# A table of 1152 scale factors, transposed on TensorE before it is written to memory

## The chip, the core and the metric

The kernel runs on one core of a Trainium2 chip. Its engines work side by side, each through its own queue in order: TensorE (PE) multiplies matrices into PSUM banks, VectorE (DVE) and ScalarE (ACT) do elementwise work, GpSimd (POOL) issues the gathers and scatters by index, SyncE (SP) issues the other transfers. All transfers run on the same 16 DMA engines. The metric is the device time of one execution in microseconds (us); lower is better.

## The reference

Attention over (2, 8, 576, 64), then a first mixture of eight experts with Sinkhorn weights, then a second mixture in which each of N = 1152 tokens goes to its best expert alone:

```
xn = x / (norm(x) + 1e-6);  en = emb / (norm(emb) + 1e-6)
logits = xn @ en.T / tau
expert_idx = argmax(logits, 1);  probs = softmax(logits)
gate_w = probs[arange(N), expert_idx]
for e in range(8):
    mask = expert_idx == e
    out[mask] = gate_w[mask, None] * (relu(x[mask] @ w1[e]) @ w2[e])
```

x has 512 columns, w1[e] is 512x1024 and w2[e] 1024x512. The change concerns the factor per token, gate_w with the kernel's own scaling, on its way to the last line.

## The kernel before, in words

The tokens lie nine to a partition (nine tiles of 128), so a number per token is a [128, 9] table. The second mixture first routes (`route`, line 1124, three groups of 384 tokens; `favourite`, line 1208, and `places`, line 1250, turn counts per expert into positions), and then computes in slots of 128 tokens that share an expert. In the profiled execution 11 slots are computed. Each token's row is written to a table in memory, `rows`, and its factor to another, `sizes`. A slot then fetches what belongs to it by index: `gather` (line 1328) its 128 rows into a tile in `nb`, `size` (line 1338) its 128 factors into a tile `sz`. Both are issued by POOL through `fetch` (line 1344). Rows of the slots 0 to 2 are turned round on PE (`transposed`, line 1102: eight small matmuls from `nb`, then one copy by ACT into a tile in `r_e`); from slot 3 on a transposing transfer on SP does it.

A slot (`slot`, line 1350) has two halves on PE. The ups multiply by w1 (96 matmuls 128x128, two PSUM banks), ACT and DVE turn their result into a high and a low fp16 half in `xa`. The downs multiply by w2 (18 matmuls 128x512 in fp16, and the last two blocks in fp32, which the trace shows as rows `r_k,xa`) into a third bank. ACT then writes the result times the token's factor (`x<-pb,sz`) and POOL scatters it to `out`. Weights come over SP (`r_st`, `r_e`, `r_k` from `in_m2w`, line 1306), skipped where the slot has the expert of the slot before, and are split into halves by ACT (high) and DVE (low) into `r_bias`, `r_q`, `r_v`, `r_e`.

`scales` (line 1192) makes the factors from row sums, the logits and their maxima: `norm_inverse`, an Exp on ACT, a sum, two reciprocals. `sizes` is needed first by the gather of slot 0's factors, and so by the end of slot 0.

The order on the engines is not the order of the code. Every call is recorded and `Plan.issue` (line 268) issues the operations of a whole stage by estimated costs and due times, keeping the best of several rounds. The first mixture, the routing and the first 11 slots are one such stage, so an added operation can move others far from it. PSUM banks are taken in turn from a ring of six (`turn_of(banks)`), slot after slot. All recorded instructions carry the line 157, so rows are told apart by their tiles.

Of the kernel before, what the change touches and what calls it, by code (L numbers as in the profile page):

```python
# [10 lines left out]
F32 = mybir.dt.float32  # L11
F16 = mybir.dt.float16
BF16 = mybir.dt.bfloat16
I32 = mybir.dt.int32
# [8 lines left out]
N, DM, E, F = 1152, 512, 8, 1024  # L23
NT = 9
# [298 lines left out]
def attn_moe_moe_kernel(ctx: ExitStack, tc: tile.TileContext, a, out):  # L323
    nc = tc.nc
    vec, act, pe, pool, sp = nc.vector, nc.scalar, nc.tensor, nc.gpsimd, nc.sync
# [4 lines left out]
    def sbuf_pool(name, bufs, stack=ctx):  # L330
        return stack.enter_context(tc.tile_pool(name=name, bufs=bufs))
# [3 lines left out]
    sml = sbuf_pool("sml", 1)  # L335
# [4 lines left out]
    vec, act, pe, pool, sp = (plan.engine(e) for e in "vatgs")  # L340
# [20 lines left out]
    def carve(t, *parts, off=0):  # L361

        out = []
        for shape, dtype in parts:
            out.append(at(t, off, shape, dtype))
            off += -(-int(np.prod(shape)) * mybir.dt.size(dtype) // 64) * 64
        return out
# [3 lines left out]
    def turn_of(ring):  # L371
        i = turns[id(ring)] = turns.get(id(ring), -1) + 1
        return ring[i % len(ring)]
# [72 lines left out]
    def take(n):  # L446
        nonlocal o
        o += n
        return cst[:, o - n:o]

    ident, upper, desc8, iotas = take(128), take(128), take(8), take(SLOTS)
    steps, lower8, iota128, numbers = take(72), take(64), take(128), take(18).rearrange("p (t i) -> p t i", i=2)

    def tt(eng, out, in0, in1, op=ALU.add):
        eng.tensor_tensor(out=out, in0=in0, in1=in1, op=op)
# [14 lines left out]
    def warm(ps, n):  # L470
# [10 lines left out]
        out=sst, in0=w2r.unsqueeze(1).to_broadcast([128, 4, H]), in1=blk4.unsqueeze(2).to_broadcast([128, 4, H]),  # L481
# [568 lines left out]
    def norm_inverse(nrm, inv, ss, tmp):  # L1050

        rsqrt(inv, tmp, ss, 3)
        tt(vec, nrm, ss, inv, ALU.mult)
        vec.tensor_scalar(nrm, nrm, 1e-6, None, ALU.add)
        vec.reciprocal(inv, nrm)

    zr = at(hss[1], 2048, [DM], I32)[0:1]
    emb, upper16, ones16, rank, st2, lt, order8, wk, w8, w16, en = carve(
        r_e, ([DM], F32), ([128], F16), ([128], F16), ([NT, E], F32), ([8, NT], F32), ([3, NT, E], F32),
        ([E, E], F32), ([NT, E], F32), ([E, E], F32), ([2, SLOTS, E], F32), ([KD, E], F32), off=r_sml)  # L1060
# [4 lines left out]
    rows = drp.tile([N + 1, DM], I32, name="rows")  # L1065
    sizes = drp.tile([N + 1, 1], I32, name="sizes")
    szs = [sml.tile([128, 1], I32, name=f"sz{i}") for i in range(4)]
    seen = sml.tile([128, E], F16, name="seen")
    oh = sml.tile([128, NT, E], F16, name="oh")
    fav = sml.tile([128, 3, E], F32, name="fav")  # L1070
# [121 lines left out]
    def scales():  # L1192

        norm_inverse(st2[:, 1], st2[:, 6], st2[:, 0], st2[:, 7])
        l = lt[:, 2]
        tt(vec, l, lt[:, 0], st2[:, 4].unsqueeze(2).to_broadcast([128, NT, E]), ALU.subtract)
        tt(vec, l, l, st2[:, 6].unsqueeze(2).to_broadcast([128, NT, E]), ALU.mult)
        act.activation(l, l, ACTF.Exp)
        vec.tensor_reduce(out=st2[:, 7], in_=l, axis=AX.X, op=ALU.add)
        vec.tensor_scalar(st2[:, 7], st2[:, 7], 1e-9, C_XN * C_W * C_W, ALU.add, ALU.mult)  # L1200
        tt(vec, st2[:, 7], st2[:, 7], st2[:, 2], ALU.mult)
        vec.reciprocal(st2[:, 7], st2[:, 7])
        with nc.allow_non_contiguous_dma(reason="a number per token"):
            sp.dma_start(out=sizes[0:N, 0].rearrange("(t p) -> p t", p=128), in_=st2[:, 7].bitcast(I32))

    got, xn_early = [], []

# [179 lines left out]
    mps, banks = [scs[2][:, 0:512]], [scs[0][:, 0:512], scs[1][:, 0:512], pab, pO]  # L1387
# [50 lines left out]
    for _ in route(2):  # L1438
        pass
    scales()  # L1440
    got += [xn_early[0], size(0)]

# [65 lines left out]
```

## Time and profile before

| | before |
|---|---|
| median of three runs | 1100.46 us (1097.18 to 1105.92) |
| the profiled execution | 1098.71 us, of it span 1096.9 us |
| PE busy, of the span | 1027.2 us, 94% |
| DVE, ACT, POOL busy | 842.3, 702.4, 288.6 us |
| mean granted TensorE clock | 0.976 |

A row of the timeline has start, duration, engine, line, operation, and the tiles as out<-in with shape and count. A bracket at its end gives the engine's idle time just before it and what ended that. In the stage tables each engine has its busy time with the count of instructions; PEclk is the granted share of TensorE's 2.4 GHz, so 0.50 is the lower level, 1.2 GHz.

### The profile page before, as it was taken

To read this page: it belongs to the slowest core of one execution; us is meant where nothing else is said; L and a number is where in the kernel's file an instruction comes from. 1 tells how busy PE (TensorE), PEld (TensorE's weight loads), DVE (VectorE), ACT (ScalarE), POOL (GpSimd) and SP (SyncE) were. 2 spreads that over 40 slices of the span, in tenths; PEclk is the share of its full clock that TensorE was granted. 3 is DMA by queue.
4 is the path that set the end of the run, shared out by engine and by line. 5 is a ranking of instruction groups with operands and counts; after the bars stand their busy time and mean duration, and the time that the engine had idled before them with its cause. 6 is when DMAs were issued, how large, how long until landed. Compare 5 with 4: busy or idle time off the path is not lost. (4 is left out here: it accounts for less than half of the span.)

```text
span 1096.9 us, 28775 instructions
## 1 busy us (share of the span) xinstructions
PE 1027.2 (94%) x11973; PEld 909.2 (83%) x11973; DVE 842.3 (77%) x1366; ACT 702.4 (64%) x1119; POOL 288.6 (26%) x233
## 2 busy tenths in 40 slices
PE   6787999999899999999999999999999999859896
PEld 2344666799899999999999999999999999636563
DVE  7887888756767697787787787887887887957882
ACT  6777999931436467576576576566666665657872
POOL 3452000001642132232332232222322210154221
PEclk9789999999999999999999999999999999979999
DMA  8644234200577057257357357348345023257693
GB/s 279 180 141 124 54 78 110 95 2 19 149 177 172 14 141 167 64 136 169 67 128 174 68 119 169 78 112 178 79 122 114 2 85 117 70 96 212 184 295 101
DMA packets 79472, 132.71 MB, mean 121 GB/s; under 512 B 19030, under 2 KB 40222, under 8 KB 79080
## 3 DMA queue, kind: packets, MB, share of 16 engines
q1 hardware_dynamic: 61432, 95.94, 28.5%
q0 software_dynamic: 17904, 34.88, 18.3%
q8 instruction: 95, 1.56, 0.6%
q14 instruction: 41, 0.34, 0.1%
HBM read 111.87 MB, written 5.29 MB: 107 GB/s over the span
## 5 line engine op out<-in xcount | busy, mean ns | idle before, releaser
L157 PEld LDWEIGHTS <-r_bias 128*128 128x128 f16 x4920 | 400.5, 98 | 7.3 <-issue 6.6
L157 PEld LDWEIGHTS <-r_v 128*128 128x128 f16 x2880 | 235.7, 98 | 6.8 <-issue 5.7
L157 PE MATMUL pb<-r_k,r_bias 128*128 128x192 f16 x2304 | 205.0, 247 | 0.5 <-ACT r_e L157 0.5
L157 POOL TENSOR_TENSOR r_q<-r_w,r_q 128x768 f16<-128x768 f32 (+1 forms) x54 | 107.7, 1994 | 268.4 <-ACT r_q L157 262.3
L157 PE MATMUL pb<-nb,r_v 128*128 128x192 f16 x1260 | 151.4, 246 | 0.7 <-ACT r_e L157 0.7
L157 PE MATMUL pb<-r_q,r_bias 128*128 128x192 f16 x1512 | 132.8, 246 | 0.0
L157 PE MATMUL pb<-nb,r_e 128*128 128x192 f16 x756 | 103.6, 246 | 0.0
L157 PE MATMUL pb<-xa,r_v 128*128 128x192 f16 x1008 | 99.5, 246 | 0.0
L157 PEld LDWEIGHTS <-r_e 128*128 128x128 f16 x1139 | 95.7, 98 | 1.2 <-issue 1.1
L157 ACT ACTIVATE r_e<-pb 128x384 f32<-128x384 f32 (+1 forms) x96 | 48.1, 504 | 63.8 <-PE pb L157 63.3
L157 ACT ACTIVATE r_w<-pb 128x384 f32<-128x384 f32 x96 | 46.5, 487 | 54.9 <-PE pb L157 54.4
L157 PEld LDWEIGHTS <-r_q 128*128 128x128 f16 (+1 forms) x560 | 41.4, 101 | 43.0 <-issue 21.2
L157 POOL DMA_DIRECT2D r_st<-r_st x42 | 42.3, 1008 | 116.0 <-DMA r_st<-in_m1w 49.9
L157 DVE TENSOR_TENSOR r_q<-r_w,r_q 128x384 f16<-128x384 f32 (+1 forms) x46 | 65.4, 1421 | 5.2 <-ACT r_q L157 5.1
L157 DVE CUSTOM_DVE_ANT_0 r_e<-sc,nb 128x576 f32<-128x576 f32 x72 | 53.7, 754 | 15.0 <-PE sc L157 11.8
L157 ACT ACTIVATE r_bias<-r_bias,r_w 128x576 f32<-128x576 f32 x72 | 59.5, 859 | 8.6 <-DVE r_bias L157 3.4
L157 POOL DMA_DIRECT2D r_e<-r_e x42 | 41.2, 980 | 87.3 <-DMA r_e<-in_m1w 43.2
L157 ACT ACTIVATE r_q<-r_w 128x1152 f16<-128x1152 f32 x50 | 57.8, 1156 | 4.8 <-DMA r_w<-in_qT 4.8
L157 ACT ACTIVATE r_e<-r_e,mn 128x576 f32<-128x576 f32 x72 | 55.4, 770 | 8.4 <-DVE mn L157 8.1
L157 PE MATMUL pab<-r_bias,r_w 128*32 128x288 f32 x472 | 46.6, 446 | 14.1 <-DVE r_bias L157 11.0
L157 DVE SCALAR_TENSOR_TENSOR r_bias<-r_st,r_bias 128x1024 f16<-128x1024 f32 (+1 forms) x45 | 50.5, 1138 | 11.8 <-ACT r_bias L157 11.6
L157 ACT ACTIVATE r_bias<-r_st 128x1024 f16<-128x1024 f32 (+1 forms) x45 | 43.4, 985 | 21.6 <-PE pb L157 17.8
(238 smaller groups left out, 1990.9 us busy)
## 6 DMA issues: line engine op xcount, KB each, us to landing
r_k<-in_m2w SPq DMA_DIRECT2D x48, 512.0 KB
r_st<-in_m2w SPq DMA_DIRECT2D x24, 512.0 KB
r_e<-in_m2w SPq DMA_DIRECT2D x24, 512.0 KB
r_st<-in_m1w SPq DMA_DIRECT2D x22, 512.0 KB
r_st<-in_m1w SPq DMA_DIRECT2D x42, 256.0 KB
r_e<-in_m1w SPq DMA_DIRECT2D x42, 256.0 KB
r_e<-in_m1w SPq DMA_DIRECT2D x14, 512.0 KB
r_st<-r_st POOLq DMA_DIRECT2D x14, 512.0 KB, 6.3
```

The lines of the kernel that those rows point to most:

```text
L157: self.add(e, lambda: f(*a, **k), cost, dma, ins, outs, port)
```

## The change

The [128, 9] table of factors is first transposed on PE into a bank of the ring, as [9, 128]; DVE copies it to a new tile `szt`, and SP writes that: nine runs of 128 numbers, 512 bytes each. Before, SP wrote straight from the [128, 9] table, where neighbours in a row lie 512 bytes apart in memory: 1152 runs of 4 bytes. What stands in memory is the same.

```
     szs = [sml.tile([128, 1], I32, name=f"sz{i}") for i in range(4)]
+    szt = sml.tile([NT, 128], F32, name="szt")
...
         vec.reciprocal(st2[:, 7], st2[:, 7])
-        with nc.allow_non_contiguous_dma(reason="a number per token"):
-            sp.dma_start(out=sizes[0:N, 0].rearrange("(t p) -> p t", p=128), in_=st2[:, 7].bitcast(I32))
+        ps = turn_of(banks)[0:NT, 0:128]
+        pe.transpose(ps, st2[:, 7], ident)
+        vec.tensor_copy(szt, ps)
+        sp.dma_start(out=sizes[0:N, 0].rearrange("(t p) -> t p", p=128), in_=szt.bitcast(I32))
```

The transpose takes one bank of the ring, so every slot's banks move on by one, and the planner's order changes too. Three places matter.

PE, from the end of the routing to the first rows of slot 2. `pb<-r_w,x` are the nine matmuls of `places` from which every later index follows, `pb<-r_e,...` the ups of slot 1, `pb<-r_bias,xa` its downs, `pb<-r_e,nb` the turning of slot 2's rows. Before:

```order
L157 MATMUL pb_3114<-r_e,r_bias 128x128
L157 LDWEIGHTS x_70
L157 MATMUL pb_3115<-r_w,x_70 128x36
L157 LDWEIGHTS xa
L157 MATMUL pb_3109<-r_bias,xa 128x512
...
L157 MATMUL pb_3109<-r_k_76,xa 128x512 x2
L157 LDWEIGHTS nb_72
L157 MATMUL pb_3116<-r_e,nb_72 128x128
```

The same place now (`pb_3111<-r_e 9x128` is the new transpose, `pb_3114<-r_k_76,xa` the end of slot 0's downs):

```order
L157 MATMUL pb_3114<-r_k_76,xa 128x512
L157 LDWEIGHTS x_70
L157 MATMUL pb_3116<-r_w,x_70 128x36
L157 LDWEIGHTS r_q
L157 MATMUL pb_3115<-r_e,r_q 128x128
...
L157 MATMUL pb_3111<-r_e 9x128
...
L157 LDWEIGHTS nb_72
L157 MATMUL pb_3117<-r_e,nb_72 128x128
...
L157 LDWEIGHTS xa
L157 MATMUL pb_3111<-r_bias,xa 128x512
```

The nine matmuls have moved from the end of slot 1's ups to a place before them, beside slot 0's downs (which moved behind the counting of the routing), and slot 2's rows are turned before slot 1's downs instead of after them.

ACT, where it copies slot 2's turned rows (`r_e<-pb 128x1024`). Before:

```order
L157 ACTIVATE xa<-pb_3114 128x256
L157 ACTIVATE r_bias<-r_st 128x2x512
L157 ACTIVATE r_q<-r_st 128x2x512
L157 ACTIVATE r_q<-r_e 128x2x512
L157 ACTIVATE r_v<-r_e 128x2x512
L157 ACTIVATE r_e<-pb_3116 128x1024
L157 ACTIVATE r_v<-r_k_75 128x2x512 x3
```

And now:

```order
L157 ACTIVATE xa<-pb_3110 128x256
L157 ACTIVATE r_e<-pb_3117 128x1024
L157 ACTIVATE r_bias<-r_st 128x2x512
L157 ACTIVATE r_q<-r_st 128x2x512
L157 ACTIVATE r_q<-r_e 128x2x512
L157 ACTIVATE r_v<-r_e 128x2x512
L157 ACTIVATE r_v<-r_k_75 128x2x512 x3
```

The copy has moved ahead of the four splits of slot 2's w1.

SP, where it writes the table (ISA rows set registers). Before:

```order
L1306 DMA r_e<-in_m2w 128x1024
L157 DMA sizes<-r_e 128x9x1
L1306 ISA
L1306 DMA r_k_75<-in_m2w 128x2x512
L1306 ISA
```

And now:

```order
L1309 DMA r_e<-in_m2w 128x1024
L1309 ISA
L1309 DMA r_k_75<-in_m2w 128x2x512
L157 DMA sizes<-szt 9x128
L1309 ISA
```

The write stands one weight load later. On POOL the gathers keep their order up to slot 3's factors: two early gathers of rows, seven more, then the factors of the slots 0 to 3.

## Rows read from the trace of the kernel before

**Rows 1.** Stages of the span: length, then busy time of the engines.

```profile
300.00:929.00 629.00, 625.72 (x7571) 624.14 (x7569) 496.21 (x609) 389.05 (x580) 176.91 (x131) 1.00 0.49 115
929.00:986.00 57.00, 41.57 (x465) 31.99 (x462) 42.09 (x114) 34.85 (x54) 17.98 (x14) 0.88 0.42 89
986.00:1087.00 101.00, 94.18 (x956) 64.15 (x954) 76.17 (x75) 70.25 (x91) 27.87 (x19) 0.98 0.70 209
```

**Rows 2.** Timeline of PE, from slot 1's turned rows to slot 2's downs.

```profile
948.73 0.62 PE L157 MATMUL pb<-r_e,nb 128*128 128x128 f16 x8 [2.23 <-DMA nb<-rows,idx_early]
950.46 0.33 PE L157 MATMUL pb<-r_e,r_q 128*128 128x128 f16 x3 [1.11 <-ACT r_e L157]
...
956.29 4.04 PE L157 MATMUL pb<-r_bias,xa 128*128 128x512 f16 x18
960.17 1.88 PE L157 MATMUL pb<-r_k,xa 128*128 128x512 f32 x4
970.56 1.04 PE L157 MATMUL pb<-r_e,nb 128*128 128x128 f16 x8 [8.51 <-DMA nb<-rows,idx]
972.71 0.48 PE L157 MATMUL pb<-r_e,r_bias 128*128 128x128 f16 x3 [1.11 <-ACT r_e L157]
...
981.98 2.42 PE L157 MATMUL pb<-r_v,xa 128*128 128x512 f16 x6 [2.38 <-ACT x L157]
```

**Rows 3.** Timeline of POOL: gathers of rows for slots 1 and 2.

```profile
944.47 1.87 POOL L157 DMA_INDIRECT nb<-rows,idx_early  x1 [28.13 <-DVE r_e L157]
957.48 1.00 POOL L157 DMA_INDIRECT nb<-rows,idx  x1 [11.14 <-ACT xa L157]
```

**Rows 4.** Timeline of SP: three row stores ahead of slot 1's gather; the table's write.

```profile
937.64 3.83 SPq L157 DMA_DIRECT2D rows<-nb  x3
...
957.64 0.39 SPq L157 DMA_DIRECT2D sizes<-r_e  x1
```

**Rows 5.** Packets from 958 to 960 us by queue: packets, MB, share of 16 engines.

```profile
q0 software_dynamic: 7, 0.03, 113.1%
q1 hardware_dynamic: 1168, 0.00, 26.2%
```

**Rows 6.** All packets from 960 to 962 us.

```profile
DMA packets 0, 0.00 MB, mean 0 GB/s; under 512 B 0, under 2 KB 0, under 8 KB 0
```

**Rows 7.** All packets from 962 to 969 us.

```profile
DMA packets 56, 0.20 MB, mean 29 GB/s; under 512 B 7, under 2 KB 7, under 8 KB 56
```

**Rows 8.** All packets from 972 to 973 us.

```profile
DMA packets 125, 0.39 MB, mean 389 GB/s; under 512 B 30, under 2 KB 30, under 8 KB 125
```

**Rows 9.** PE alone in two stretches: length, PE busy, granted clock.

```profile
965.25:975.49 10.24, 3.81 (x35) 0.50 0.77 163
982.32:985.73 3.41, 3.41 (x10) 0.50 0.21 79
```

**Rows 10.** Timeline of DVE: first and last step of the chain that makes the indices.

```profile
946.62 0.16 DVE L157 COPY fav<-pb 128x8 f32<-128x8 f32 x1
...
956.55 0.19 DVE L157 TENSOR_SCALAR idx<-pb 128x36 int32<-128x36 f32 x1
...
956.88 0.21 DVE L157 RECIPROCAL r_e<-r_e 128x9 f32<-128x9 f32 x1
```

**Rows 11.** Timelines of PE and DVE: another table transposed and copied earlier in the kernel.

```profile
269.27 0.27 PE L157 MATMUL sc<-r_e 128*72 128x128 f32 x1
...
269.58 0.29 DVE L157 COPY r_e<-sc 72x128 f32<-72x128 f32 x1 [0.68 <-PE sc L157]
```

**Rows 12.** Timelines of ACT (copy and three splits) and DVE (one split).

```profile
971.64 1.02 ACT L157 ACTIVATE r_e<-pb 128x1024 f16<-128x1024 f16 x1 [10.73 <-PE pb L157]
972.56 2.94 ACT L157 ACTIVATE r_v<-r_k 128x1024 f16<-128x1024 f32 x3
...
958.10 1.22 DVE L157 SCALAR_TENSOR_TENSOR r_bias<-r_st,r_bias 128x1024 f16<-128x1024 f32 x1 [0.52 <-ACT r_bias L157]
```

**Rows 13.** Waits of ACT from 986 to 1087 us, the largest for weights: total, times, longest.

```profile
ACT r_v L157 <- DMA r_e<-in_m2w: 3.5, 4, 1.9
```

## Prediction: what the transposed table does to the time

> **What bounds the kernel now.** I read the stages first [rows 1]. From 300 to 929 us, the bulk of the first mixture, PE is busy 625.72 of 629.00 us: whatever the changed order does there, it can win at most 3.3 us. From 986 us to the last slot PE is busy 94.18 of 101.00 us. Between them lies the one loose stretch, 929 to 986 us, where the routing ends and the slots begin: 41.57 of 57.00 us, 15.4 us idle.
>
> PE's timeline names these 15.4 us [rows 2]. Five waits make 15.3 of them: 2.23 for slot 1's gathered rows, 1.11 for their copy, 8.51 for slot 2's rows, 1.11 for their copy, 2.38 for ACT's scaling of slot 0. The reader is to see the 8.51: PE has finished slot 1's downs at 962.05 (960.17 + 1.88) and starts the next matmul at 970.56.
>
> Why are slot 2's rows late? POOL issued their gather at 957.48; slot 1's gather, issued at 944.47, let PE go on at 948.73 [rows 2, 3]. The same 256 KB took 13.1 us (970.56 - 957.48) against 4.3. Between the issue and the data of the slow one lies SP's write of the table at 957.64 [rows 4]. The queues show what it does. From 958 to 960 us 1168 packets of at most 512 bytes start on SP's queue, and 7 packets of the gather are recorded with 113.1% of 16 engines' time over 2 us: 1.131 x 32 / 7 = 5.2 us each, where they overlap the write [rows 5]. Then not one packet starts for 2 us [rows 6], for the next 7 us the engines move 29 GB/s [rows 7], and at 972 us they move 389 GB/s [rows 8]. The gathers queued by then cannot fill that time: seven would be 1.8 MB, five microseconds at that rate. The engines look as if they wait for 1152 writes of 4 bytes to be finished, and everybody behind them waits too.
>
> The stall costs more than its length. TensorE's granted clock is 0.50, the 1.2 GHz level, from 965.25 to 975.49, with 3.81 us of work in it, and again from 982.32 to 985.73 with 3.41 us, after PE had idled 8.51 and then 2.38 us [rows 2, 9]. At 2.4 GHz these 7.22 us would have been half: 1.9 and 1.7 us lost.
>
> **The change part by part.** Nothing else is taken out: the 1152 runs become nine of 512 bytes. SP's sequencer spent 0.39 us on the old write; this is not on the path.
>
> *The stall.* With the write gone, the gather should take the 4.3 us of slot 1's. The new order also asks for it differently: the nine matmuls that end in `idx` stand before slot 1's ups, the rows are turned right after these ups. From `idx` to the gather's issue it took 0.93 us (956.55 to 957.48) [rows 3, 10], so the rows are there 5.2 us after `idx`; slot 1's ups take 950.46 to 956.29, 5.8 us less a few tenths for the matmuls woven into them [rows 2]. So the wait goes to about nothing: -8.5, and -1.9 for the clock after it.
>
> *The moved index chain.* From the first counts on DVE to `idx` it is 9.9 us (946.62 to 956.55) [rows 10]. Before, slot 1's turned rows and ups and 3.3 us of waits lay beside it. Now PE has only slot 0's downs (5.8 us, as slot 1's: 956.29 to 962.05) and the turned rows of slot 1 (0.6 us): 9.9 - 6.4 = 3.5 us of waiting, in which the wait for slot 1's gather is contained, plus about 1 us by which the counting, moved forward, waits for DVE. An estimate from these rows: 4.5 us instead of 3.3, +1.2. Bounds: -1 (DVE's chain loses the few operations that the new order puts behind it) and +3.
>
> *The new operations.* A transpose of 72 columns took 0.27 us on PE, its copy 0.29 us on DVE after 0.68 us of waiting [rows 11]; this one has 9 columns. PE pays +0.3. The write follows later by about a microsecond, but it is short: the last of three stores of rows ended its issue at 941.47 and the gather that needs it began at 944.47, so 256 KB in full rows were visible 3.0 us later [rows 3, 4]. The factors' gathers stand behind seven gathers of rows on POOL, so they find them there.
>
> *ACT's moved copy.* The copy (1.02) now precedes four splits (0.98 each on ACT, 1.2 on DVE) that slot 2's ups need [rows 12]. Copy, first ACT split, four DVE splits: 1.0 + 1.0 + 4.8 = 6.8 us, beside 5.8 us of slot 1's downs. PE waits about 1.0 where it waited 1.11 for the copy: 0 (-1 to +1).
>
> *The end of slot 0.* The 2.38 us before slot 2's downs stand for ACT's scaling, which came late because ACT had stood 10.73 us behind the copy [rows 2, 12]. Now ACT reaches it after the copy, nine splits and one half of the ups' result, some 11 us after the turned rows; PE has downs, that 1 us and ups beside it, 12 us. I keep 0.5: -1.9, and -1.7 for the second slow clock. But a wait of 3.5 us ahead of slot 1's ups may itself bring a slow stretch of 3.4 us, which costs 1.7; I charge half, +0.9.
>
> *Given back.* -8.5 - 1.9 + 1.2 + 0.3 + 0 - 1.9 - 1.7 + 0.9 = -11.6. The later slots do not all move up with it. ACT already waits for weights there, 3.5 us in its largest group [rows 13], and an order that is now bound by loads has only 6.8 us of idle PE in which to absorb them [rows 1]. Bounds 0 and 4; I take +1.8, the middle of a guess on the low side. That leaves -9.8 us. The first mixture's order changes in small pieces; with PE 99.5% busy and no wait to take I count 0, within 1.5.
>
> The profiled execution had 1098.71 us (span 1096.9 and 1.8 around it), 1.75 under the median of 1100.46. From the one the sum gives 1088.9, from the other 1090.7. I say **1090.5 us**, its own range 1087 to 1094.
>
> **The page that speaks against it.** The Trainium skill, "DMA: Bandwidth & Descriptors", section "Queues, rings and completion order", says that each engine goes round-robin between the queues it has work for, a packet at a time. By that rule the gather would have been held up only by packets' own time, and the first rival below follows; here 7 packets of the gather stand for 5.2 us each instead. The Trainium skill, same page, section "Back-pressure in remote DMA", says that stalled writes stall the source engine's other queues too; it is written for transfers between cores, and the silent 2 us [rows 6] agree with it.
>
> **The rivals.**
> *The write is innocent.* Its 1168 packets took 26.2% of 16 engines over 2 us, 0.5 us per engine [rows 5]; taken as what it costs, the 13.1 us belong to seven gathers issued in a row, and the new order only moves them. Then slot 2's rows come 13 us after `idx` and PE waits some 8 us, before slot 1's downs instead of after. Gain 0 to 2: 1099. For it: recorded packet time. Against it: 29 GB/s with nothing else to move [rows 7], and full rate as soon as that ends [rows 8].
> *The gain is given back in the slots.* The stall was also time in which ACT, DVE and the loads fell behind nobody. If the loads of the later slots now come late by 4.2 us more in sum than the 1.8 that I charge, 1090.5 + 4.2: 1095.
> *More than that.* No slow clock ahead of slot 1, nothing given back: 1.8 + 0.9 + up to 1.2: 1086.
> *Slower: PE waits for its new transpose.* It stands in PE's queue after 72 of slot 1's 96 ups, so all that follows waits for the last reciprocal. That came 0.33 us after `idx` [rows 10]; in the new order two splits stand between on DVE, 2.4 us more, against some 4 us of ups (72 of 96, 5.5 in all): 1.3 us of slack. If Exp or those splits make it late by more than that, every further microsecond is PE's; from 11 us on the gain is gone, and 22 us late (22 - 1.3 - 9.8 = 10.9 us more than before) it is 1% slower, 1112. Nothing in the rows is that late.
>
> **How the numbers follow.** The likeliest gets 0.60, of which 0.24 lies beyond 1% (11 us, about what a measurement of this kernel tells from no change). More than that 0.10, innocent write 0.14, given back 0.11, slower 0.05. Faster by over 1%: 0.24 + 0.10 = 0.34. Within 1%: 0.36 + 0.14 + 0.11 = 0.61. Slower: 0.05. The range 1084 to 1098 takes in the likeliest, more, and given back, and leaves out slower and most of the innocent write, under 0.2.
>
> **What would show it.** In the changed profile: no 1168 small packets, slot 2's gather about 4 us from issue to use, no 8.5 us wait before slot 2's turned rows; waits of 3 to 5 us in all around the nine `r_w,x` matmuls; slot 2's downs some 10 us earlier than 981.98; at most one stretch at 0.50 there. The sum is wrong if slot 2's rows are again 10 us or more on their way, if PE stands at `pb<-r_e 9x128`, or if the last hundred microseconds grow by more than 4.

## The result, and the profile after

The changed kernel took 1086.24 us (median of four, 1083.69 to 1088.49) where the kernel before, run beside it, took 1099.95: a ratio of 0.9874, 95% interval 0.9844 to 0.9903, some 13.7 us. Timed again in a later batch it took 1091.78 us (1086.42 to 1093.25) against 1100.84, 0.9902 (0.9868 to 0.9936), 9.1 us. It is about 1% faster; which side of 1% the two batches do not settle.

| | before | after |
|---|---|---|
| the profiled execution | 1098.71 us, span 1096.9 | 1088.49 us, span 1086.6 (the slowest of its four) |
| PE, DVE, ACT busy | 1027.2, 842.3, 702.4 us | 1025.3, 845.6, 702.1 us |
| packets under 512 B | 19030 | 17871 |
| mean granted clock | 0.976 | 0.981 |

The stages of the changed kernel, in the columns of [rows 1]:

```profile
300.00:929.00 629.00, 625.86 (x7568) 623.86 (x7567) 499.07 (x610) 389.07 (x581) 175.75 (x131) 1.00 0.49 115
929.00:986.00 57.00, 51.72 (x575) 39.76 (x573) 48.27 (x121) 40.82 (x62) 23.51 (x17) 0.91 0.34 99
986.00:1087.00 101.00, 84.93 (x848) 57.48 (x846) 69.93 (x70) 64.77 (x84) 23.45 (x17) 0.94 0.68 210
```

The first mixture is what it was (625.86 us of PE work for 625.72). The loose stretch, 929 to 986 us, now holds 51.72 us of work instead of 41.57; the stretch behind it holds less because the kernel ends earlier.

PE's timeline of the changed kernel through that stretch; it answers [rows 2]:

```profile
942.72 0.66 PE L157 MATMUL pb<-r_e,nb 128*128 128x128 f32 x4 [0.25 <-DVE r_e L157]
...
943.91 0.17 PE L157 MATMUL pb<-oh,r_e 128*128 128x8 f16 x1 [0.52 <-DVE oh L157]
...
947.72 2.72 PE L157 MATMUL pb<-r_v,xa 128*128 128x512 f16 x6 [3.37 <-DVE nb L157]
...
960.38 0.27 PE L157 MATMUL pb<-r_e 128*9 128x128 f32 x1
...
961.83 0.61 PE L157 MATMUL pb<-r_e,nb 128*128 128x128 f16 x8
962.27 4.05 PE L157 MATMUL pb<-r_bias,xa 128*128 128x512 f16 x18
...
969.27 0.28 PE L157 MATMUL pb<-r_e,r_v 128*128 128x128 f16 x2 [0.67 <-DVE r_v L157]
...
974.72 4.04 PE L157 MATMUL pb<-r_v,xa 128*128 128x512 f16 x18 [0.47 <-ACT x L157]
```

Read first the two rows without a bracket in the middle: the new transpose (`pb<-r_e 128*9`) and slot 2's turned rows at 961.83. Nothing waits there; the 8.51 us of [rows 2] are gone. Slot 2's downs start at 974.72 instead of 981.98. A new wait stands at 947.72, 3.37 us ahead of slot 0's downs.

The gathers of rows (POOL) and the table's write (SP) of the changed kernel, as in [rows 3, 4]:

```profile
944.76 1.41 POOL L157 DMA_INDIRECT nb<-rows,idx_early  x1 [27.21 <-ACT x L157]
957.09 1.74 POOL L157 DMA_INDIRECT nb<-rows,idx  x1 [10.92 <-DVE idx L157]
```

```profile
961.00 0.35 SPq L157 DMA_DIRECT2D sizes<-szt  x1
```

Slot 2's rows, asked for at 957.09, were in use at 961.83, 4.7 us later, where it had been 13.1. The index that they are fetched by, `idx`, was made as late as before, at 956.62 (DVE):

```profile
956.62 0.20 DVE L157 TENSOR_SCALAR idx<-pb 128x36 int32<-128x36 f32 x1 [2.00 <-PE pb L157]
```

The windows of the changed kernel: the stretch of [rows 7], then the stretches at half clock, as in [rows 9]:

```profile
962.00:969.00 7.00, 6.60 (x40) 3.34 (x37) 4.84 (x5) 6.97 (x9) 5.73 (x5) 1.00 0.81 230
```

```profile
938.72:942.13 3.41, 3.41 (x27) 3.35 (x26) 2.98 (x6) 3.11 (x8) 0.00 (x0) 0.50 0.43 154
945.54:952.37 6.83, 4.66 (x12) 1.58 (x12) 6.80 (x42) 2.49 (x4) 0.63 (x1) 0.50 0.43 155
```

The engines move 230 GB/s where they had moved 29. The half clock has not gone away: in this stage it has moved ahead, to the counting and slot 0's downs.

The spans differ by 10.3 us. Split at slot 2's downs: 7.26 up to there (981.98 to 974.72), 2.6 from there to ACT's last scaling, which starts at 1086.35 before and 1076.50 after (first and second row), and 0.45 in what follows.

```profile
1086.35 0.69 ACT L157 ACTIVATE x<-pb,sz 128x512 f32<-128x512 f32 x1 [3.70 <-issue]
```

```profile
1076.50 0.69 ACT L157 ACTIVATE x<-pb,sz 128x512 f32<-128x512 f32 x1 [3.70 <-issue]
```

### The profile page after: what moved, and what is told of

The parts are those of the page before. It is cut to its first block, busy times and chain, and to the rows that moved or that the text cites. A ratio compares the mean times of both kernels' runs of the same rounds, so it can differ in the third digit from the quotient of the medians.

```text
span 1086.6 us, 28773 instructions
## 1 busy us (share of the span) xinstructions
PE 1025.3 (94%) x11974; PEld 909.0 (84%) x11974; DVE 845.6 (78%) x1367; ACT 702.1 (65%) x1119; POOL 290.6 (27%) x233
## 2 busy tenths in 40 slices
DMA packets 78322, 132.71 MB, mean 122 GB/s; under 512 B 17871, under 2 KB 39072, under 8 KB 77930
## 5 line engine op out<-in xcount | busy, mean ns | idle before, releaser
L157 DVE SCALAR_TENSOR_TENSOR r_bias<-r_st,r_bias 128x1024 f16<-128x1024 f32 (+1 forms) x45 | 50.5, 1137 | 13.3 <-ACT r_bias L157 13.1
```

Of the source, the lines that this page charges most:

```text
L157: self.add(e, lambda: f(*a, **k), cost, dma, ins, outs, port)
```

## The experiments

Eleven runs follow, one of them of the changed kernel again; the four with an additional write have a table of their own further down. "Order" says whether the instructions stand in about the sequence of the kernel before or of the changed one. In the table "gather" is the time from the issue of slot 2's gather on POOL to PE's first use of its rows; where PE did not wait it is an upper bound.

| kernel | the table's write | order | median us | ratio to before | gather us | PE's wait for it |
|---|---|---|---|---|---|---|
| before | 1152 x 4 B, side by side | old | | 1 | 13.1 | 8.51 |
| runs of 36 bytes | 128 x 36 B | old | 1092.29 | 0.9934 [0.9912, 0.9956] | 4.5 | none |
| five of nine columns | 640 x 4 B, side by side | nearly old | 1100.30 | 1.0012 [0.9991, 1.0034] | 11.5 | 6.84 |
| rows of 64 bytes | 1152 x 4 B, 64 B apart | nearly old | 1087.39 | 0.9891 [0.9860, 0.9922] | 4.7 | 0.72 |
| one more turn | 1152 x 4 B, side by side | new | 1092.81 | 0.9945 [0.9923, 0.9968] | 4.6 | none |
| transpose in the other ring | 9 x 512 B | nearly old | 1091.66 | 0.9929 [0.9906, 0.9952] | 3.9 | none |
| changed, other bank for rows | 9 x 512 B | nearly old | 1092.00 | 0.9914 [0.9880, 0.9948] | 3.8 | none |
| changed, again | 9 x 512 B | new | 1091.78 | 0.9902 [0.9868, 0.9936] | 4.8 | none |

### The write alone: 128 runs of 36 bytes, in the order of before

```
-            sp.dma_start(out=sizes[0:N, 0].rearrange("(t p) -> p t", p=128), in_=st2[:, 7].bitcast(I32))
+        sp.dma_start(out=sizes[0:N, 0].rearrange("(p t) -> p t", p=128), in_=st2[:, 7].bitcast(I32))
```

> The kernel before with one line changed: the table's 1152 numbers are written as 128 runs of 36 bytes (each partition's nine together) instead of 1152 runs of 4 bytes. No transpose, no copy, and the order of all instructions on every engine is that of before. What it changes in the computation: a token gets another token's factor. Theory (the 4-byte writes hold up the engines and all that is queued behind them): slot 2's gather takes 4 to 5.5 us from issue to use instead of 13.1, the wait of 8.5 us before slot 2's turned rows shrinks to 0 to 1.5 us, the slow clock behind it goes; 6 to 12 us under the kernel before. Rival 1 (the write is innocent, the new order alone brings the gain): gather 12 to 13 us, wait 8 us, within 2 us of before. Rival 2 (the fewer packets bring the stall's end, but the last hundred microseconds give it back): the wait is gone and the time is less than 5 us under before.

POOL and PE of this kernel:

```profile
959.49 1.00 POOL L157 DMA_INDIRECT nb<-rows,idx  x1 [12.49 <-ACT xa L157]
```

```profile
963.94 0.61 PE L157 MATMUL pb<-r_e,nb 128*128 128x128 f16 x8
...
975.13 5.73 PE L157 MATMUL pb<-r_v,xa 128*128 128x512 f16 x18 [3.95 <-ACT x L157]
```

The gain was 6.9 us, with no instruction moved on any engine. The write made the stall: the innocent write falls. The 8.51 us turn into nothing at slot 2's rows; slot 2's downs start 16.6 us after `idx` (958.55) instead of 25.4. What it does not get rid of is the last wait: 3.95 us for ACT's scaling of slot 0, which waits for its factors, gathered behind seven gathers of rows.

### The order alone: one more turn of the ring, the old write kept

```
         vec.reciprocal(st2[:, 7], st2[:, 7])
+        turn_of(banks)
         with nc.allow_non_contiguous_dma(reason="a number per token"):
```

> The kernel before with one added statement that takes a turn of the ring of PSUM banks and does nothing with it, where the change puts its transpose. The old write of 1152 times 4 bytes stays; the order of the instructions and the banks of the slots become nearly those of the changed kernel. Nothing in the computation changes. Theory (the write makes the stall, the shifted banks make PE wait for `nb<-pb` ahead of slot 0's downs): the stall of 7 to 9 us for slot 2's rows stays, shown wherever the new order puts these rows, and the 3.4 us wait ahead of slot 0's downs appears too; 0 to 5 us slower than before. Rival 1 (the order and the banks bring the gain): no wait over 2 us for slot 2's rows, 8 to 14 us faster than before. Rival 2 (part by part): the order hides some of the stall and gives better later slots: 2 to 5 us faster.

SP, a window, and PE of this kernel:

```profile
964.57 0.39 SPq L157 DMA_DIRECT2D sizes<-r_e  x1
```

```profile
969.00:975.00 6.00, 3.96 (x65) 3.63 (x66) 6.00 (x7) 4.62 (x6) 0.13 (x1) 1.00 0.61 33
```

```profile
948.33 2.72 PE L157 MATMUL pb<-r_v,xa 128*128 128x512 f16 x6 [2.60 <-DVE nb L157]
...
981.22 5.45 PE L157 MATMUL pb<-r_v,xa 128*128 128x512 f16 x18 [4.53 <-ACT x L157]
```

6.4 us faster, so every expectation missed in part. The wait ahead of slot 0's downs appears as the theory said. But in the new order the factors are finished later than `idx`, and the write leaves SP 4.75 us behind slot 2's gather (964.57 after 959.82) instead of 0.16: the gather has its rows by then. The engines still stand, 33 GB/s from 969 to 975 us; weights and the gathers of factors meet it, and PE pays 4.53 us at slot 2's downs. The change therefore did two things, and either alone takes slot 2's gather out of the stall. That is why their gains, 6.9 and 6.4, need not add up; the changed kernel with both was 13.7 us faster in one batch and 9.1 in the other.

### The dose: 640 words instead of 1152

```
         sp.dma_start(out=sizes[N:N + 1], in_=zr[:, 0:1])
+        sp.dma_start(out=sizes[640:N, 0].rearrange("(o n) -> o n", o=1), in_=zr)
...
-            sp.dma_start(out=sizes[0:N, 0].rearrange("(t p) -> p t", p=128), in_=st2[:, 7].bitcast(I32))
+            sp.dma_start(out=sizes[0:640, 0].rearrange("(t p) -> p t", p=128), in_=st2[:, 7, 0:5].bitcast(I32))
```

> The kernel before with 640 of the 1152 numbers written (five of the nine columns); the other 512 entries get zeros in one 2 KB write early in the first mixture, so that the factors of the tokens from 640 on are zero. The order of instructions is near that of before. Theory (each 4-byte write costs an engine a fixed time, some 0.12 us with 72 on each of 16 engines, 8.8 us in all): 40 on each engine hold it for 4.9 us, slot 2's gather takes 9 to 9.5 us, PE's wait is 4.0 to 5.5 us instead of 8.5; 4 to 7 us under before. Rival 1 (the stall is a fixed time, whatever the count of writes): wait 7.5 to 9 us, within 2 us of before. Rival 2 (innocent write): the same as rival 1 with the gather at 12 to 13 us even though the writes are done sooner.

```profile
959.19 1.00 POOL L157 DMA_INDIRECT nb<-rows,idx  x1 [13.46 <-ACT xa L157]
```

```profile
970.64 1.04 PE L157 MATMUL pb<-r_e,nb 128*128 128x128 f16 x8 [6.84 <-DMA nb<-rows,idx]
```

My theory of a fixed price for each write falls: with 44% fewer writes the gather takes 11.5 us instead of 13.1, and the time does not move (1.0012). PE's wait of 6.84 us lies between my theory (4.0 to 5.5) and the first rival (7.5 to 9), nearer to the rival: the number of words is not what mainly counts.

### The dose, again: the same 1152 words at other distances

What 640 and 1152 words have in common is that 16 of them lie in each 64 bytes of memory. Four kernels take the 36-byte table and add a write of the same 1152 words, 4 bytes each, to a table `spare` that nobody reads; only the distance of its words differs (`[NT * 128, 1]`, `[128, NT, 2]`, `[NT * 128, 4]`, `[NT * 128, 16]` for 4, 8, 16 and 64 bytes).

```
+    spare = drp.tile([NT * 128, 16], I32, name="spare")
...
+            sp.dma_start(out=spare[:, 0].rearrange("(t p) -> p t", p=128), in_=st2[:, 7].bitcast(I32))
```

The two with 8 and 64 bytes ran first, as further tests of the count:

> The kernel before with its table written in 128 runs of 36 bytes (tokens get other tokens' factors), and ahead of it an additional write of the same 1152 numbers, 4 bytes each, 8 bytes apart, into a memory table that nobody reads. It measures what such a write costs its neighbours when nobody needs its result. Theory (many 4-byte writes hold the engines, whatever their addresses): slot 2's gather takes 11 to 14 us from issue to use. Rival 1 (what holds them is that neighbouring 4-byte words come from different engines at the same time; here the nine words of a partition lie by themselves): 4 to 6 us. Rival 2 (the gather waited for the table's result, not for engines): 4 to 6 us.

> As the run with the additional write 8 bytes apart, but each of the 1152 words lies 64 bytes from the next. Theory (count of writes): slot 2's gather again takes 11 to 14 us from issue to use. Rival (words that share a small stretch of memory wait for each other): 4 to 7 us here, whatever the run with 8 bytes shows.

Nobody needs this write, so it went out late, at 991 to 995 us, between weight loads, and slot 2's gather could not show anything. The loads did. With 8 bytes they almost stopped for 5 us, with 64 they did not, though the count was the same. So the other two:

> The kernel before with its table in 128 runs of 36 bytes (tokens get other tokens' factors), and an additional write of the 1152 numbers, 4 bytes each and side by side as in the kernel before, to a memory table that nobody reads. In the runs with the words 8 and 64 bytes apart this write was issued at 992 us, between weight loads; with 8 bytes the engines then moved 37 to 119 GB/s for 5 us (996 to 1001), with 64 bytes apart 293 to 381 GB/s, no dip. Theory (words that share a stretch of 64 bytes are written one after the other, some 0.55 us each, and everything behind them waits): 16 words share it here, a dip under 120 GB/s of 8 to 10 us. Rival 1 (a dip that depends on how many words are written, or on none of this, as the loads alone have dips there): 0 to 5 us.

> The same with the words of the additional write 16 bytes apart, so that 4 share 64 bytes. Theory (0.55 us for each word that shares the 64 bytes): a dip of about 2.2 us (1.5 to 3) behind the write, between none with 64 bytes apart and 5 us with 8. Rival 1 (only words that touch each other, or lie within some 8 bytes, hold each other up): no dip, as with 64 bytes. Rival 2 (any sharing of 64 bytes costs the same): 5 us or more.

Windows behind the additional write, with 4, 8, 16 and 64 bytes from word to word (last column GB/s; in the first kernel a stretch ahead of the dip stands above it). The last fence is the kernel with runs of 36 bytes and no additional write, at its own lowest place there and then at full rate:

```profile
996.00:998.00 2.00, 2.00 (x32) 1.76 (x31) 2.00 (x3) 1.88 (x2) 1.00 (x1) 1.00 1.04 395
1000.00:1007.00 7.00, 6.11 (x70) 4.34 (x68) 2.90 (x3) 1.20 (x2) 0.00 (x0) 1.00 0.90 40
```

```profile
996.00:1001.00 5.00, 5.00 (x58) 3.56 (x57) 2.83 (x4) 1.66 (x2) 0.00 (x0) 1.00 0.81 68
```

```profile
995.00:998.00 3.00, 3.00 (x45) 2.48 (x44) 2.58 (x4) 1.65 (x2) 0.00 (x0) 1.00 1.02 210
```

```profile
995.00:996.00 1.00, 1.00 (x7) 0.52 (x5) 1.00 (x2) 0.79 (x2) 0.00 (x0) 1.00 1.15 142
996.00:1001.00 5.00, 5.00 (x59) 3.60 (x58) 3.99 (x5) 2.87 (x3) 0.00 (x0) 1.00 0.96 333
```

```profile
991.00:994.00 3.00, 3.00 (x12) 1.35 (x10) 3.00 (x3) 2.51 (x3) 0.81 (x1) 1.00 1.29 143
996.00:1001.00 5.00, 3.82 (x66) 3.47 (x64) 2.62 (x3) 3.54 (x4) 2.69 (x3) 1.00 1.03 386
```

| distance of the words | words in 64 bytes | what the loads show | the one execution |
|---|---|---|---|
| 4 bytes | 16 | 40 GB/s for 7 us | 1101.94 us |
| 8 bytes | 8 | 68 GB/s for 5 us | 1094.30 us |
| 16 bytes | 4 | 210 GB/s for 3 us | 1088.27 us |
| 64 bytes | 1 | 142 GB/s for 1 us, then 333 | 1088.40 us |

The dip gets longer and deeper the closer the words lie, in one execution of each. The expected law (0.55 us per word that shares the 64 bytes: 8.8, 4.4, 2.2 and next to nothing) holds for 4 and 8 bytes, about: 7 us instead of 8.8, 5 instead of 4.4. For 16 bytes it is not shown: 210 GB/s for 3 us is no lower than the 143 GB/s for 3 us that the loads have by themselves in the kernel without the write, and the same goes for the 142 GB/s for 1 us with 64. With 8 bytes the neighbours are nine words of one partition, with 4 bytes words of 16 partitions; both stall. In the kernel with 4 bytes ACT waited 8.98 us for weights behind the write, and PE 6.18 us for ACT (rows of ACT and of PE):

```profile
1011.18 1.06 ACT L157 ACTIVATE r_v<-r_e 128x1024 f16<-128x1024 f32 x1 [8.98 <-DMA r_e<-in_m2w]
```

```profile
1012.29 0.29 PE L157 MATMUL pb<-r_e,r_v 128*128 128x128 f16 x1 [6.18 <-ACT r_v L157]
```

Whether the stretch that counts is 64 bytes, 32 or more was not measured; 64 is a distance that is enough. Nor was distance parted from the stretch of memory that the whole table covers: 4.6 KB at 4 bytes, 9.2 at 8, 18.4 at 16, 73.7 at 64. That many small writes into a few kilobytes are slow, whether or not any two share 64 bytes, is a rival that no run here excludes; 128 runs of 36 bytes in the same 4.6 KB did not stall the gather.

### The same 1152 writes, each in its own 64 bytes, where they are needed

```
-    sizes = drp.tile([N + 1, 1], I32, name="sizes")
-    szs = [sml.tile([128, 1], I32, name=f"sz{i}") for i in range(4)]
+    sizes = drp.tile([N + 1, 16], I32, name="sizes")
+    szs = [sml.tile([128, 16], I32, name=f"sz{i}") for i in range(4)]
...
+        sp.dma_start(out=sizes[0:N].rearrange("(o a b) c -> o a (b c)", o=1, a=36),
+                     in_=zr.unsqueeze(1).to_broadcast([1, 36, DM]))
...
-        return sz.bitcast(F32)
+        return sz.bitcast(F32)[:, 0:1]
```

> The kernel before with the table's rows 64 bytes wide instead of 4: still 1152 writes of 4 bytes from the same tile, but each into its own 64 bytes; the gathers fetch 64 bytes a token (zeros behind the number, written early by one transfer). Nothing is computed otherwise, nothing transposed. Theory (the stall is for words that share 64 bytes, not for the count of small writes): slot 2's gather takes 4 to 6 us from issue to use instead of 13.1, no wait over 2 us before slot 2's turned rows, 5 to 9 us under before, as with runs of 36 bytes (1092). Rival 1 (1152 small writes on a path that is needed at once cost what they cost, and the dip at 992 us was another thing): gather 11 to 14 us, the wait of 7 to 9 us stays, within 3 us of before. Rival 2 (the wider gathers of factors cost what is gained): the wait is gone, the time within 3 us of before.

SP, POOL and PE of this kernel:

```profile
957.88 0.39 SPq L157 DMA_DIRECT2D sizes<-r_e  x1
```

```profile
958.03 1.00 POOL L157 DMA_INDIRECT nb<-rows,idx  x1 [11.10 <-DVE r_e L157]
```

```profile
962.77 0.62 PE L157 MATMUL pb<-r_e,nb 128*128 128x128 f16 x8 [0.72 <-DMA nb<-rows,idx]
...
972.07 3.37 PE L157 MATMUL pb<-r_v,xa 128*128 128x512 f16 x14 [0.38 <-ACT x L157]
```

The gather leaves 0.15 us behind the write, where it left 0.16 us ahead of it before, and takes 4.7 us. 1152 writes of 4 bytes on the same path at the same moment cost the gather nothing that shows, once no two share 64 bytes. The rival of the count falls for good. It ran 11.4 us faster than before, 0.9891, as fast as the changed kernel without transpose, copy or shifted banks, and more than the 5 to 9 us that I expected.

The surplus over the run with 36 bytes (6.9 us) is not shown to be the write's. The planner put only six gathers of rows ahead of slot 0's factors here instead of seven, so these are asked for at 967.83 instead of 971.26 (first row: 64 bytes, second: 36), and PE waits 0.38 us before slot 2's downs instead of 3.95.

```profile
967.83 1.96 POOL L157 DMA_INDIRECT sz<-sizes,idx_early  x1 [0.30 <-issue]
```

```profile
971.26 1.42 POOL L157 DMA_INDIRECT sz<-sizes,idx_early  x1 [0.30 <-issue]
```

### The new wait: is the bank to blame?

The transpose takes a turn of the ring of banks, so slot 0's downs write to the bank in which route(2)'s third block of rows still stands; DVE reads it (`<-DVE nb`). One kernel puts the transpose in the other ring; one leaves it and moves that block instead.

```
-        ps = turn_of(banks)[0:NT, 0:128]
+        ps = turn_of(mps)[0:NT, 0:128]
```

> The changed kernel with its transpose in a bank of the other ring, that of the small matmuls, so that the banks of the slots are those of before. The computation is that of the changed kernel. Theory (PE's 3.4 us wait ahead of slot 0's downs is for the bank that the shifted ring shares with the rows' sums, and the slow clock of 938 to 952 us belongs to the waits and half-speed work there): the wait is under 1 us and the kernel 1 to 4 us faster than the changed one, 14 to 18 us under before. Rival 1 (the wait is for something else that ends at that time, or only moves to the next matmul): same time as the changed kernel within 1 us. Rival 2 (the shifted banks are what gave the 2.6 us in the later slots): 1 to 4 us slower than the changed kernel, with the gain of the later slots gone.

```
-        ring = [banks[(turns[id(banks)] - i) % 6] for i in range(3)] if g == 2 else mps
+        ring = [banks[(turns[id(banks)] - i) % 6] for i in (0, 1, -1)] if g == 2 else mps
```

> The changed kernel with one number changed: the last routing group transposes its third block of rows in the bank after the current turn instead of the one two before it. Nothing in the computation changes; slot 0's downs find their bank free and stand ahead of the counting. Theory (PE's 3.4 us wait ahead of slot 0's downs, and the half-speed clock around it, are the price of the bank that the shifted ring shares with these rows): wait under 0.5 us, 2 to 6 us faster than the changed kernel, 1080 to 1085 us. Rival 1 (PE must wait for the counting chain anyway, so the wait only moves to the nine `r_w,x` matmuls or to slot 1's rows): within 1.5 us of the changed kernel. Rival 2 (the new order loses elsewhere, as when the transpose was put in the other ring): 3 to 6 us slower than the changed kernel.

PE of the second one, and the row of ACT ahead of its slot 2's downs:

```profile
951.24 0.62 PE L157 MATMUL pb<-r_e,nb 128*128 128x128 f16 x8 [1.32 <-DMA nb<-rows,idx_early]
952.97 0.33 PE L157 MATMUL pb<-r_e,r_q 128*128 128x128 f16 x3 [1.11 <-ACT r_e L157]
956.86 0.20 PE L157 MATMUL pb<-r_w,x 128*128 128x36 f16 x2 [1.05 <-DVE r_w L157]
...
977.23 5.73 PE L157 MATMUL pb<-r_v,xa 128*128 128x512 f16 x18 [3.95 <-ACT r_e L157]
```

```profile
975.27 0.38 ACT L157 ACTIVATE xa<-pb 128x256 f16<-128x256 f32 x1 [3.09 <-remote]
```

The wait goes with the bank: both kernels lose it, and neither has the half clock between 938 and 952 us. But neither is faster than the changed kernel (0.9929 and 0.9914; 0.9902 for it in the second's batch). The 3.4 us come back as 1.32, 1.11 and 1.05 us for slot 1's rows, their copy and the index chain. The 3.95 us before the second one's slot 2's downs are another matter: ACT had just stood 3.09 us behind something that the profile does not name (`<-remote`), and the kernel with the transpose in the other ring has 2.05 us there.

My theory that the bank's wait costs 2 to 6 us falls; the first rival, that the wait only moves, fits. It is not the only one left. With the bank free the planner also went back to nearly the old order, on PE the same in both kernels but for a few matmuls, so bank and order changed together. And the later slots take 104.1 us with the transpose in the other ring, where the changed kernel's took 101.8 and 97.8, as the second rival for it has it.

### The changed kernel again

> The changed kernel once more, timed in one batch with the others. Expected by what was measured: 1083 to 1089 us, 1.0 to 1.6% under before. If short write and new order each bring about 7 us by themselves (before with runs of 36 bytes: -6.9; before with one more turn of the banks: -6.4), their sum is -13.3 and this run should show it; if they are two ways to the same gain, it should be no more than 8 us under before.

9.1 us under before, and outside the 1083 to 1089 us that I expected: between the two cases written down, so whether the gains add up stays open. Its profiled execution (span 1091.5) shows how much one execution can say (PE, then ACT):

```profile
950.12 2.72 PE L157 MATMUL pb<-r_v,xa 128*128 128x512 f16 x6 [3.38 <-DVE nb L157]
...
969.07 2.38 PE L157 MATMUL pb<-r_bias,xa 128*128 128x512 f16 x10 [0.62 <-issue]
...
983.37 4.04 PE L157 MATMUL pb<-r_v,xa 128*128 128x512 f16 x18 [0.47 <-ACT x L157]
```

```profile
969.24 0.66 ACT L157 ACTIVATE xa<-pb 128x256 f16<-128x256 f32 x2 [6.57 <-remote]
```

The waits at slot 0's and slot 2's downs are the same, yet slot 2's downs start 8.65 us later than in the first profile. 2.4 us of this are there at slot 0's downs; 5.7 arise between slot 2's turned rows and its downs, 18.6 us instead of 12.9. There ACT stood 6.57 us behind something that the profile does not name, PE stood 1.5 us in four pieces with no wait to show for it (`<-issue`) and 2.4 us for splits that DVE had late, and a stretch at half clock followed (976.13 to 979.55). ACT's last scaling comes only 4.6 us later (1081.14 against 1076.50). So a mark in the middle of one profile is good to several microseconds, and part of a delay there is caught up behind it.

## Why the prediction was right, and where not

I predicted 1090.5 us with a range of 1084 to 1098; 1086.24 and 1091.78 were measured, one below and one inside its own range of 1087 to 1094. Against its own profiled execution the sum gave 1088.9, and the profiled execution after took 1088.49. The likeliest course, the stall gone and a fair part of the gain kept, came. That the sum met the profiled execution so closely is luck: up to slot 2's downs my terms gave a gain of 9.9 us and 7.3 came; behind them they gave a loss of 0.1 and a gain of 3.0 came. The two misses cancel. By the first batch the change passes 1%, which I had given 0.34. Not all terms that made the sum were right.

**The stall (-8.5, and -1.9 for the clock behind it): right in size.** Rows 5.2 us after `idx` were predicted; PE used them 5.2 us after it (961.83 - 956.62), without a wait. The half clock of 965 to 975 us is gone.

**Its cause: half right.** "They wait for 1152 writes of 4 bytes to be finished" is right in that the write stops the queues behind it, as the 36-byte run shows. It does not say why these writes are slow, and taken as a matter of their count, as I first tested it, it is wrong: 640 words stall nearly as long, 1152 words 64 bytes apart not at all. What holds the engines are words written close together in memory; whether sharing 64 bytes or the small stretch of the whole table does it was not parted. The Trainium skill, "DMA: Bandwidth & Descriptors", section "Specifications", says that below 512 bytes a DMA does read-modify-write; by size alone every variant here with 4 or 36 bytes would be alike. The runs disagree: 4.7 us with 4 bytes apart by 64, 13.1 with 4 bytes side by side. A read-modify-write that must wait for its neighbour's would fit, but that is argued, not shown. The rule that I had set against the change, from the Trainium skill, "DMA: Bandwidth & Descriptors", section "Queues, rings and completion order", would hold the gather up by packet time alone; the stalled runs do not agree, with 13.1 us for the gather where the small packets' recorded time was 0.5 us per engine [rows 5]. The Trainium skill, same page, section "Back-pressure in remote DMA", by which stalled writes stall the engine's other queues too, agrees with them better, though it is written for transfers between cores and this one is local.

**The index chain (+1.2: 4.5 us of waits instead of 3.3): right in size, wrong in place.** The waits were 0.25, 0.52 and 3.37 us, 4.1 in all. I had put them at the `r_w,x` matmuls and slot 1's rows. They stood at slot 0's downs, for a bank. I had read the shift of the ring in the order of instructions and not asked who still reads the bank that each slot now gets. In the run with the other bank the waits there are 3.5 us in all: about the same sum, in other places.

**The transpose (+0.3, no wait), ACT's copy (0), the end of slot 0 (0.5 us left of 2.38): right.** PE's rows show 0.27 us without a wait, no wait at all for the copy but 0.67 for a split on DVE, and 0.47 us. The slower rival, PE standing at its transpose, did not come.

**The half clock (+0.9): the term that was mis-sized.** I had charged half of one stretch. Two came, at 938.72 and 945.54, with 3.41 and 4.66 us of work in them. Half of that, 4.0 us, is the most that they can cost. The first lies ahead of the 3.37 us wait that DVE ended, and DVE had waited only 0.77 us for PE there (row below), so I estimate 0.8 of its 1.7 us as lost, and 0.8 + 2.3 = 3.1 in all.

```profile
942.51 0.16 DVE L157 COPY r_e<-pb 128x3 f32<-128x3 f32 x1 [0.77 <-PE pb L157]
```

That is 2.2 us more than charged, and with the 0.67 us for a split most of why slot 2's downs came 7.3 us earlier where my terms up to there gave 9.9 (8.5 + 1.9 - 1.2 - 0.3 + 1.9 - 0.9). The kernel run again and the one with one more turn show two such stretches between 939 and 956 us too; the two kernels without the bank's wait show none there.

**Given back in the later slots (+1.8) and the second half clock (-1.7): the clock right, the giving back wrong in sign.** Instead of about nothing, this part brought 2.6 us. From slot 2's downs to the last scaling it took 104.4 us before and 101.8 after, for the same 966 matmuls. Before, two stretches at half clock lie in it, after, one (PE busy, then the granted clock):

```profile
982.32:985.73 3.41, 3.41 (x10) 1.22 (x8) 2.82 (x4) 3.41 (x5) 2.40 (x2) 0.50 0.21 79
1033.52:1036.93 3.41, 3.02 (x8) 0.77 (x9) 3.41 (x4) 3.41 (x6) 1.21 (x2) 0.50 0.54 149
```

```profile
1003.57:1006.98 3.41, 3.28 (x7) 1.45 (x7) 3.41 (x4) 3.41 (x4) 0.00 (x0) 0.50 0.02 3
```

Half of 6.43 us of work less half of 3.28 is 1.6 us: the stretch that I had counted on went. PE's idle time in this part fell from 6.2 to 5.6 us, so nothing was given back where I had charged 1.8. Whether the change did this is open. The second profile of the changed kernel took 97.8 us for this part, the kernel with one more turn 98.0; in nearly the old order it took 104.1 with rows of 64 bytes, 105.1 with runs of 36, but also 100.8 with five of nine columns and 100.7 and 101.5 with the additional write 64 and 16 bytes apart. The work at half clock in it goes from none to 9.5 us, PE's idle time from 1.9 to 8.1. One profile of each kernel, with 4 us between two of the same, cannot tell what sets them.

**The rivals.** The innocent write is out by the 36-byte run. Given back (1095) and slower did not come. "More than that" (1086) gave the first batch's number, but not by its reason: the slow clock ahead of slot 1 was there.

## What to carry to other kernels

Before writing a table of single numbers, look where neighbours in memory come from: give each number its own 64 bytes, or make longer runs, of 36 bytes here; transposing on TensorE is one way. A wider row needs no transpose and was here as good (11.4 us against 13.7 and 9.1); a change of index order, tried only with the factors in the wrong places, brought 6.9. A slow transfer may be somebody else's: look at what all queues moved in its time. And where a change takes a turn of a ring, list who holds the buffer that each later step now gets.

## What the runs showed of the hardware

A write of 1152 four-byte words that nobody reads cut the loads of all queues from 395 to 40 GB/s for 7 us when the words lay side by side; 8 bytes apart it was 68 GB/s for 5 us. With 16 and 64 bytes there was nothing beyond what the loads show without such a write (210 GB/s for 3 us, 142 for 1 us; 143 for 3 us without). The same 1152 words on the path of a gather of 256 KB held it for 13.1 us when they lay side by side; 64 bytes apart the gather took 4.7 us, as in the changed kernel, which has nine runs of 512 bytes. The records of the writes themselves show none of it: in the kernel before, 1168 packets took 26.2% of 16 engines for 2 us [rows 5], and the silence comes after them.
